# Batch 0 of a Fourier mixing and a gated feed-forward block: half-size even sums, another order of loads, joins and E copies in the head of the kernel

## The chip, the cores and the metric

The kernel runs on one core of one Trainium2 chip. The metric is the device time in microseconds (us) of one execution: the median of three runs before the change is 1908.64 us (1908.24 to 1908.96). A core has TensorE (PE, with the weight load PEld beside it), VectorE (DVE), ScalarE (ACT), GpSimd (POOL) and SyncE (SP), which here issues nearly all of the transfers, and 16 DMA engines.

## What is computed

```python
def _attn_ref(x):                       # x: (8, 3008, 256), float32
    X = np.fft.fft(x, axis=1)
    X = np.fft.fft(X, axis=2)
    return X.real.astype(np.float32)

def _moe_ref(x, w_gate, w_val, w_out):  # x: (24064, 256); d_ff = 1536
    gate = 1.0 / (1.0 + np.exp(-(x @ w_gate)))
    val = x @ w_val
    return (gate * val @ w_out).astype(np.float32)
```

The second takes the result of the first, reshaped to rows of 256. The three weights arrive as float64 and are converted on the chip.

## The kernel before, in words

The transform over the sequence is done with cosine and sine tables (`stab`, held in SBUF as `ST[0]` and `ST[1]`, 128 partitions x 6 sets q x 753 columns: 377 for even frequencies, 376 for odd ones). The rows of a batch are first folded on VectorE (`fold_ops`, `half_rows` for batch 0), so that 128 x 6 points remain; point number 6p + q lies in partition p and set q. TensorE then sums over the partitions, once per set: 128 feature columns as weights, 377 or 376 table columns as the moving operand. Sums over even sets go to one PSUM bank (`ev`) and over odd sets to another (`od`). `places` writes their sum to the low frequencies and their difference to the mirrored high ones (`ends` 0 and 1). The results are `pk` (cosine) and `qk` (sine). The one feature column that is its own mirror, "E", gets its own sums with one-column weights, whose outputs lie in four groups of 32 partitions of one PSUM bank (`e_sums`); its row goes to the DRAM tensor `ed`, and is read back broadcast to all partitions as `ek` (`e_load`, `e_rows`).

The feature transform is not applied to the data: it is merged into the gate and value weights. For each of 18 weight blocks, `weight_load` brings 0.5 MB of float64; `weight_parts` (two ACT operations), `weight_join` (two `tensor_scalar` and one `scalar_tensor_tensor` on VectorE, one add on GpSimd) make float32 of it; `weight_use` calls `merge`, which is four matmuls with the table `dt` into a bank `ps` and two ACT copies to `G2` and `G1`, each block giving two of the 12 hidden chunks of gate or value. One first row of `G2` per hidden chunk goes to `ge`.

Then comes the main loop, one step i per batch, frequency chunk of 252 and hidden chunk of 128 (576 steps). A step multiplies `pk` (`front_a`) and `qk` (`front_b`) with `G1` and `G2` into a bank `pf` with two halves, gate and value; for the first five steps E is added by a matmul with the row `e0`, from step 5 on an ACT operation seeds the bank with `ek` times `ge`. `gate_a` and `gate_b` make the gated product `h` on ACT and VectorE; `back` multiplies it with the output weights into `po` banks, five steps later. In the first 13 steps, the blocks of weights not yet merged are converted and merged beside this.

All queues are written out by hand, in program order for each engine: the scheduler is manual, so an engine does its instructions in the order in which the code names them, and waits on semaphores for what they read. `at(i, f)` puts a piece of work behind step i; `gap`, `pre`, `join`, `use` and `spare` put it at other places of a step. At most eight of SP's transfers are in flight: the ninth waits for the first.

The head, before step 0, is what the change rewrites. Its order before: load weight blocks 0 and 1, then rows and tables of sets 0 and 1, 2 and 3, 4, 5 (`load_rows`, `load_table`, L192 and L195), with the odd columns of the sine table last; convert and merge blocks 0 and 1; fold, sum and place set by set in the order of `SLICES`; convert blocks 2 and 3; the places of E, cosine and sine.

Of the kernel before, what the change touches and what calls it, by code (L numbers as in the profile page):

```python
# [8 lines left out]
F32 = mybir.dt.float32  # L9
# [3 lines left out]
ALU = mybir.AluOpType  # L13
# [40 lines left out]
NQ = 6  # L54
NP = 128
# [26 lines left out]
def kernel(  # L82
# [10 lines left out]
    nc = tc.nc  # L93
    B, _, _, _, D = xf.shape
    F = moe_w_gate.shape[1]
# [36 lines left out]
    def mm(o, l, r, start, stop):  # L132
        nc.tensor.matmul(o, l, r, start=start, stop=stop, skip_group_check=True)  # L133

    def bank(name, other=None):
        if other is not None:
            return pso.tile([P, 512], F32, name=name, tag=f"po{other}")
        return psx.tile([P, 512], F32, name=name, tag="x")
# [49 lines left out]
    table = const.tile([2, 1], F32, name="table")  # L188
    ed = dram.tile([B, NK + 1], F32, name="ed")

    def load_rows(q, n):
        nc.sync.dma_start(out=X[0][0:NP, :, q : q + n], in_=xf[0, :, :, q : q + n])  # L192

    def load_table(t, q, n, lo=0, hi=NE + NO):
        nc.sync.dma_start(out=ST[t][0:NP, q : q + n, lo:hi], in_=stab[:, t, q : q + n, lo:hi])  # L195

    NQ4 = NE // 4 + 1
    TILES = [(g, par, par * HP + g * TB) for g in range(2) for par in range(2)]
# [199 lines left out]

    WO = {}

    turns = itertools.count()

    def weight_use(j):
        w, c = jobs[j]
        if w == 2:
            WO[c] = WS.pop(j)
        else:
            merge(WS.pop(j), w, c, (4, 2, 3)[next(turns) % 3] if j > 1 else None)

    def merge(ws, g, c, other):  # L410
        cs = slice(c * WC, (c + 1) * WC)
        ps = bank("ps", other)
        for h in range(2):
            for t in range(2):
                mm(ps[:, h * WC : (h + 1) * WC], dt[:, t, h * HD : (h + 1) * HD], ws[:, t, :],
                   h == 0 and t == 0, t == 1)
        nc.scalar.copy(G2[:, g, cs], ps[:, WC : 2 * WC])
        nc.scalar.copy(G1[:, g, cs], ps[:, 0:WC])
        for f in range(c * WC // P, (c + 1) * WC // P):
            nc.sync.dma_start(  # L420
                out=ge[:, g, f : f + 1], in_=G2[0:1, g, f * P : (f + 1) * P])
# [60 lines left out]
    TURN = {}  # L482
    MORE = {}

    SLICES = ((0, 1), (2, 3), (4,), (5,))

    def fold_ops(b, nq):
        x4 = X.pop(b)
# [82 lines left out]
        else:  # L571

            def half_rows(q):
                even, odd = slice(0, 4, 2), slice(1, 4, 2)
                point(nc.vector, even, odd, q)
                first(nc.vector, even, odd, q)
                for blk in range(2):
                    across(nc.vector, blk, q)
                v, r = x4[:, 0:2, q], x4[:, 2:4, q]
                for to, op in ((r, ALU.subtract), (v, ALU.add)):  # L580
                    nc.vector.tensor_tensor(to[:, :, :, 1:HD], v[:, :, :, 1:HD], v[:, :, :, D - 1 : HD : -1],
                                            op=op)
                nc.vector.memset(r[:, :, :, 0:1], 0.0)
            ops += [lambda q=q: half_rows(slice(q[0], q[-1] + 1)) for q in SLICES]
        for blk, (v, r) in enumerate(parts):
            if b and blk:
                W[b, blk] = v[:, :, HD:D], r[:, :, HD:D]
# [4 lines left out]

    PQE = {}

    def half(b, w, d, blk, sn, other=None):


        c0, n = ((0, NE), (NE, NO))[blk]
        ev, od = [bank(name, other and other[i])[:, 0:n] for i, name in enumerate(("ev", "od"))]

        def sums(*qs):
            for q in sorted(qs, key=lambda q: q % 2):
                mm((ev, od)[q % 2], w(q), ST[int(sn)][0:NP, q, c0 : c0 + n], q < 2, q >= NQ - 2)

        def then():
            a = evp.tile([P, NE], F32, name="a", tag="a")[:, 0:n]
            nc.scalar.copy(a, ev)
            return lambda: places(d, blk, sn, a, od)
        return sums, then

    def places(d, blk, sn, ev, od, ends=(0, 1)):
        if 0 in ends:
# [64 lines left out]
        for t in PQE[b]:  # L677
            nc.vector.memset(t[:, NK:], 0.0)

    def seq_group(b, blk, what, other=None):  # L680
        return half(b, lambda q: W[b, blk][what][:, q, :], PQE[b][what], blk, what == 1, other)


    def e_load(b):
        nc.sync.dma_start(out=x8[:, b - 1], in_=xf[b, :, :, :, HD : HD + 1])

# [4 lines left out]
        tt(x8[:, :, 1], x8[:, :, 0], x8[:, :, 2], op=ALU.add)  # L691
        tt(x8[:, :, 3], x8[:, :, 0], x8[:, :, 2], op=ALU.subtract)

    E0 = []

    def e_sums(m=B - 1):


        ps = bank("pe", NB - 1)
        at_ = lambda blk, par: slice((2 * blk + par) * TB, (2 * blk + par) * TB + m)  # L700

        def sums(*qs):
            for q in qs:
                for blk in range(2):
                    c0, n = ((0, NE), (NE, NO))[blk]
                    w = x8[:, :, 1 + 2 * blk, q] if m > 1 else W[0, blk][2][:, q]
                    mm(ps[at_(blk, q % 2), 0:n], w, ST[0][0:NP, q, c0 : c0 + n], q < 2, q >= NQ - 2)

        def even():
            er = op.tile([P, NK + 1], F32, name="er", tag="os")[0:m]  # L710
            if m == 1:
                E0.append(er)
            nc.vector.memset(er[:, NK:], 0.0)
            if m > 1:
                a, e1 = (evp.tile([P, NE], F32, name="a", tag="a")[0:m] for _ in range(2))
                o1 = a
            else:
                a, e1 = (zp.tile([P, 2 * CH], F32, name="z", tag="z")[0:m, 0:NE] for _ in range(2))
                o1 = app.tile([P, 2 * CH], F32, name="ae", tag="ae")[0:m, 0:NE]
            nc.scalar.copy(a, ps[at_(0, 1), 0:NE])  # L720
            nc.scalar.copy(e1[:, 0:NO], ps[at_(1, 0), 0:NO])

            places(er, 0, True, a, ps[at_(0, 0), 0:NE])

            def rest():
                nc.scalar.copy(o1[:, 0:NO], ps[at_(1, 1), 0:NO])

            def last():
                places(er, 1, False, e1[:, 0:NO], o1[:, 0:NO], (0,))

            def end():
                places(er, 1, False, e1[:, 0:NO], o1[:, 0:NO], (1,))
                nc.sync.dma_start(out=ed[1:] if m > 1 else ed[0:1], in_=er)
            return rest, last, end
        return sums, even

    def e_joint():
        sums, even = e_sums()
        sums(*range(NQ))
        return even()  # L740

# [206 lines left out]
    nc.gpsimd.memset(nil, 0.0)  # L950
    nc.scalar.activation(table, nil[:, 0, 0:1], AF.Sigmoid)
    nc.gpsimd.dma_start(out=zero, in_=nil)
    nc.scalar.dma_start(out=dt, in_=dtab.rearrange("(c p) d -> p c d", p=P))
    load_x(0)
    for j in range(2):
        weight_load(j)
    load_rows(0, 2)
    load_table(0, 0, 2)
    load_rows(2, 2)
    load_table(1, 0, 2, 0, NE)  # L960
    load_table(0, 2, 2)
    load_rows(4, 1)
    load_table(0, 4, 1)
    load_rows(5, 1)
    weight_load(2)
    load_table(1, 2, 2, 0, NE)
    load_table(0, 5, 1)
    load_table(1, 4, 2, 0, NE)
    load_table(1, 0, NQ, NE)
    for j in (3, 5, 6, 8, 9, 4, 7):  # L970
        weight_load(j)

    e0 = shared["qk"][:, 4 * WC : 4 * WC + CH]
    nc.gpsimd.memset(e0, 0.0)
    weight_parts(0)
    weight_parts(1)
    weight_join(0)
    weight_join(1)
    warm = bank("warm", 2)
    for i in range(4):  # L980
        mm(warm[:, 0:WC], dt[:, 0, 0:P], dt[:, 0], True, True)
    weight_use(0)
    weight_use(1)
    seq_start(0)

    cos = [seq_group(0, blk, 0, (2 * blk, 2 * blk + 1)) for blk in range(2)]
    e_, e_even = e_sums(1)
    sin = [seq_group(0, 0, 1)]
    for q, f in zip(SLICES, fold_ops(0, 2), strict=True):
        f()  # L990
        e_(*{1: (0, 1), 5: (2, 3, 4, 5)}.get(q[-1], ()))
        sin[0][0](*{5: (3,)}.get(q[-1], ()))
        cos[0][0](*q)
        cos[1][0](*q)
        sin[0][0](*{1: (0, 1), 4: (2,), 5: (4, 5)}.get(q[-1], ()))
    places_c = [cos[blk][1]() for blk in range(2)]
    weight_parts(2)
    weight_join(2)
    rest, *ends = e_even()
    rest()  # L1000
    for f in ends:
        f()
    for f in places_c:
        f()
    nc.scalar.copy(e0[0:1], E0[0][:, 0:CH])
    weight_parts(3)
    weight_join(3)
    sin.append(seq_group(0, 1, 1, (0, 1)))
    sin[1][0](*range(NQ))
    for j in range(KEEP, KEEP + 3):  # L1010
        weight_load(j)
    places_s = [group[1]() for group in sin]
    for f in places_s:
        f()
    e_rows(0)

    per = NFT * len(chunks)
    side, mid, gap, spare = {}, {}, {}, {}

    def at(i, *fs):  # L1020
        side.setdefault(i, []).extend(fs)
# [21 lines left out]
    for i, f in zip((1, 2, 2, 2, 3, 4, 4, 4, 5, 6, 6, 8, 8, 8, 9, 9, 9, 9, 10, 10, 10, 11, 11), quarter_x(1), strict=True):  # L1043
        at(i, f)
    at(i0 + 1, lambda: load_x(1))
    for b in range(1, B):
        at(20 + b, lambda b=b: e_load(b))
    at(3 * i0, e_fold)
# [37 lines left out]
    def first_ends():  # L1086
        one, two = quarter_ends(1, 1), quarter_ends(1, 0)
        for i, f in zip((55, 65, 65, 66, 66, 67, 67, 68, 68, 69, 69, 70, 70, 71, 71, 72, 73, 74, 75, 76),
                        one[0] + two[0] + one[1] + two[1], strict=True):
            gap.setdefault(i, []).append(f)  # L1090
    at(16, first_folds)
    at(3 * i0 + 14, lambda: seq_start(1))
    for blk in range(2):
# [152 lines left out]
```

## Time and profile before

| | us |
|---|---|
| median of three runs | 1908.64 |
| the profiled execution | 1909.15 |
| its span | 1907.4 |
| PE busy in the span | 1895.6 |
| first matmul of the first `pf`, from the span's start | 33.05 |
| VectorE, ScalarE, GpSimd busy | 1520.6, 1353.2, 1543.4 |

The granted clock is full throughout. Times in the profile count from the span's start. "L133" is the helper `mm`, so matmuls are told apart by their tiles; one call of `mm` shows as two instructions, and "x8" is four calls.

### The profile page before, as it was taken

To read this page: it belongs to the slowest core of one execution; us is meant where nothing else is said; L and a number is where in the kernel's file an instruction comes from. 1 tells how busy PE (TensorE), PEld (TensorE's weight loads), DVE (VectorE), ACT (ScalarE), POOL (GpSimd) and SP (SyncE) were. 2 spreads that over 40 slices of the span, in tenths; PEclk is the share of its full clock that TensorE was granted. 3 is DMA by queue.
4 is the path that set the end of the run, shared out by engine and by line. 5 is a ranking of instruction groups with operands and counts; after the bars stand their busy time and mean duration, and the time that the engine had idled before them with its cause. 6 is when DMAs were issued, how large, how long until landed. Compare 5 with 4: busy or idle time off the path is not lost.

```text
span 1907.4 us, 36057 instructions
## 1 busy us (share of the span) xinstructions
PE 1895.6 (99%) x11836; PEld 1756.6 (92%) x11836; DVE 1520.6 (80%) x3375; ACT 1353.2 (71%) x3235; POOL 1543.4 (81%) x2733
## 2 busy tenths in 40 slices
PE   8999999999999999999999999999999999999999
PEld 5788999999999999999999999999999999999998
DVE  7678888878979778897788878888788777977775
ACT  4777777777777777777777777677767777777775
POOL 2489879987999779997799878999789986877770
PEclk9999999999999999999999999999999999999999
DMA  8446221212022121211211212122120110010001
GB/s 315 120 134 80 71 89 51 72 33 81 21 64 54 31 87 32 62 41 37 89 39 48 45 39 81 40 52 58 30 74 17 36 37 15 15 25 17 15 18 30
DMA packets 197333, 109.33 MB, mean 57 GB/s; under 512 B 134823, under 2 KB 188818, under 8 KB 195354
## 3 DMA queue, kind: packets, MB, share of 16 engines
q1 hardware_dynamic: 196568, 106.50, 21.1%
q8 instruction: 95, 1.56, 0.3%
q14 instruction: 92, 0.75, 0.1%
q10 hardware_dynamic: 546, 0.51, 0.1%
q0 software_dynamic: 32, 0.00, 0.0%
HBM read 71.24 MB, written 47.87 MB: 62 GB/s over the span
## 4 chain that ended last, share of the span: by engine, by line
PE 94%; DMA 2%; SPq 1%; POOL 1%; ACT 1%; DVE 0%; issue 0%; ACTq 0%; POOLq 0%
PE pf L133 49%; PE po L133 41%; PE sum L133 2%; DMA rtab<-in_stab_dram 1%; PE ps L133 1%; POOL sf L824 1%; DMA st<-in_stab_dram 1%; SPq L206 1%; DMA raw<-in_moe_w_val_dram 0%; PE od L133 0%; POOL x L507 0%; SPq L192 0%; SPq L375 0%; PE pe L133 0%; PE ev L133 0%
## 5 line engine op out<-in xcount | busy, mean ns | idle before, releaser
L824 POOL TENSOR_TENSOR sf<-h,sf 128x168 f32<-128x168 f32 (+1 forms) x1104 | 621.0, 582 | 79.5 <-DVE h L818 75.9
L824 POOL TENSOR_TENSOR sf<-h 128x168 f32<-128x168 f32 (+1 forms) x920 | 519.3, 584 | 159.8 <-DVE h L818 158.0
L133 PE MATMUL pf<-qk,G 128*128 128x252 f32 (+1 forms) x2304 | 583.4, 376 | 0.9 <-ACT ae L787 0.8
L133 PE MATMUL pf<-pk,G 128*128 128x252 f32 (+1 forms) x2304 | 582.7, 376 | 0.0
L772 ACT ACTIVATE pf<-ek,ge 128x252 f32<-128x252 f32 (+1 forms) x1142 | 538.2, 471 | 23.2 <-DMA ge<-G 3.0
L133 PE MATMUL po<-sf,wf 128*128 128x168 f32 (+1 forms) x2944 | 508.3, 305 | 0.0
L787 ACT ACTIVATE ae<-pf 128x504 f32<-128x504 f32 (+1 forms) x576 | 338.8, 588 | 218.7 <-PE pf L133 217.2
L133 PEld LDWEIGHTS pf<-pk,G 128*128 128x128 f32 x2304 | 435.9, 190 | 53.3 <-ACT pf L772 1.5
L133 PE MATMUL po<-h,wf 128*128 128x168 f32 (+2 forms) x2584 | 461.3, 307 | 0.0
L133 PEld LDWEIGHTS po<-sf,wf 128*128 128x128 f32 x2944 | 453.4, 190 | 8.0
L818 DVE TENSOR_TENSOR h<-pf,z 128x252 f32<-128x252 f32 (+1 forms) x576 | 240.4, 417 | 274.0 <-ACT pf L815 270.5
L802 DVE TENSOR_TENSOR z<-ae,pf 128x504 f32<-128x504 f32 (+1 forms) x576 | 384.6, 668 | 83.1 <-ACT h L801 79.1
L908 DVE TENSOR_TENSOR c<-c 128x168 f32<-128x168 f32 (+1 forms) x920 | 438.7, 500 | 3.3
L133 PEld LDWEIGHTS pf<-qk,G 128*128 128x128 f32 x2304 | 410.6, 190 | 32.3 <-ACT ae L787 2.1
L133 PEld LDWEIGHTS po<-h,wf 128*128 128x128 f32 x2584 | 410.4, 190 | 17.8 <-issue 0.9
L801 ACT ACTIVATE h<-pf 128x252 f32<-128x252 f32 (+1 forms) x576 | 216.9, 376 | 146.3 <-PE pf L133 129.0
L815 ACT ACTIVATE pf<-z 128x252 f32<-128x252 f32 (+1 forms) x576 | 214.3, 372 | 116.4 <-DVE h L814 114.5
L814 DVE TENSOR_TENSOR h<-h,pf 128x252 f32<-128x252 f32 (+1 forms) x576 | 232.9, 404 | 0.0
L824 POOL TENSOR_TENSOR sf<-sf 128x168 f32<-128x168 f32 (+1 forms) x184 | 101.7, 553 | 14.4
L824 POOL TENSOR_TENSOR sf<-sf,h 128x168 f32<-128x168 f32 (+1 forms) x184 | 110.1, 598 | 0.0
L891 ACT COPY c<-po 128x504 f32<-128x504 f32 (+1 forms) x138 | 78.5, 569 | 0.0
L918 DVE STREAM_TRANSPOSE os<-c 128x256 f32<-128x256 f32 x188 | 76.5, 427 | 0.1
(158 smaller groups left out, 876.4 us busy)
## 6 DMA issues: line engine op xcount, KB each, us to landing
x<-xr SPq DMA_DIRECT2D x14, 1536.0 KB
out_dram<-os SPq DMA_DIRECT2D x376, 56.0 KB
xr<-in_xf_dram SPq DMA_DIRECT2D x105, 128.0 KB
x<-x SPq DMA_DIRECT2D x112, 96.0 KB
xr<-in_xf_dram SPq DMA_DIRECT2D x14, 384.0 KB
ek<-ed SPq DMA_DIRECT2D x40, 126.0 KB
out_dram<-os SPq DMA_DIRECT2D x288, 7.0 KB
xr<-in_xf_dram SPq DMA_DIRECT2D x21, 124.0 KB
```

What stands on the lines that cost most here:

```text
L133: nc.tensor.matmul(o, l, r, start=start, stop=stop, skip_group_check=True)
L772: nc.scalar.activation(PF[i][:, g], EK[i // NFT], AF.Copy, scale=ge[:, g, f : f + 1])
L787: nc.scalar.activation(AP[i], PF[i], AF.Copy, scale=2.0)
L801: nc.scalar.activation(H[p][:, fh, 0:n], PF[i][:, 0], AF.Sigmoid)
L802: nc.vector.tensor_tensor(z[:, :, ::-1], AP.pop(i), PF[i], op=ALU.subtract)
L814: nc.vector.tensor_tensor(h[:, fh, 0:n], h[:, fh, 0:n], pf[:, 1], op=ALU.mult)
L815: nc.scalar.activation(pf[:, 0], z[:, 0], AF.Sigmoid)
L818: nc.vector.tensor_tensor(h[:, fh, n:], pf[:, 0], z[:, 1], op=ALU.mult)
L824: nc.gpsimd.tensor_tensor(block(p, dst), block(p, a), block(p, b), op=(ALU.subtract, ALU.add)[op])
L891: (nc.vector.tensor_copy if t == 1 or t == 3 else nc.scalar.copy)(C[0][:, 3 * t * R : 3 * (t + 1) * R], PO[t][:, 0 : 3 * R])
L908: nc.vector.tensor_tensor(t[:, dst * R : (dst + 1) * R], *v, op=(ALU.subtract, ALU.add)[op])
L918: nc.vector.transpose(os_[0][0][:, s, 0:nb, h, :], t[:, c0 : c0 + nb * TB])
```

## The change

The even sets are split by the mirror symmetry of the tables. Partitions with even number hold the rows of their own set; in partitions with odd number the rows of sets 0 and 2 are swapped by the loads (`load_rows`, in halves of 64 partitions), and likewise half of the table columns (`load_mixed`). A sum over set 0 or set 2 then gives, for 189 or 188 columns, only one of two banks x and y; set 4 is summed twice with a table that is zero in the partitions of the other parity (`apart`, in part of `wf`). `unfolded` makes the 377 and 376 even sums of them, with an add and a subtraction; `places` follows as before. E's sums are made in the same way (`e_first`).

The order of the head changes with it. Rows and tables of the even sets come first, as half tables, then sets 5, 1 and 3, then `dt` and the weight blocks. Warm-up matmuls run on zeros in place of `dt`. The unfolding and the low places of cosine come first, then the joins of blocks 0 and 1, then E, the sine unfolding, `e0`, the join of block 2 and the places of `qk`. E's sums are copied to free parts of `G1` and `G2`. Five of the mirrored places (`qk` of the first part, two of E, two of `pk`) move into steps 1 to 3, and with them E's store and the first `e_rows`. At step 35 `load_again` brings the whole even sets of the cosine table, which batches 1 to 7 need for E.

```diff
-    def load_rows(q, n):
-        nc.sync.dma_start(out=X[0][0:NP, :, q : q + n], in_=xf[0, :, :, q : q + n])
+    def load_rows(*qs):
+        for q in qs:
+            for ps, r in ((slice(0, NP, 2), q), (slice(1, NP, 2), 2 - q)) if q in (0, 2) else ((slice(0, NP), q),):
+                nc.sync.dma_start(out=X[0][ps, :, q], in_=xf[0, ps, :, r])
+    H0, H1 = NE // 2, NE + NO // 2
+    def load_table(t, q):
+        nc.sync.dma_start(out=ST[t][0:NP, q], in_=stab[:, t, q])
+    def load_mixed(t):
+        for ps, qs in ((slice(0, NP, 2), slice(0, 3, 2)), (slice(1, NP, 2), slice(2, None, -2))):
+            nc.sync.dma_start(out=ST[t][ps, 0:3:2, H0:H1], in_=stab[ps, t, qs, H0:H1])
+    def load_apart():
+        for h in range(2):
+            nc.sync.dma_start(
+                out=wf.rearrange("p g m n -> p g (m n)")[h:NP:2, h::2, 6 * WC : 6 * WC + NE], in_=stab[h::2, :, 4, H0:H1])
+    def load_again():
+        nc.sync.dma_start(out=ST[0][0:NP, 0:NQ:2], in_=stab[:, 0, 0:NQ:2])
...
-    SLICES = ((0, 1), (2, 3), (4,), (5,))
+    SLICES = (slice(4, 5), slice(0, 3, 2), slice(5, 6), slice(1, 2), slice(3, 4))
...
+    def unfolded(f, x, y, sn=False):
+        nc.vector.tensor_tensor(f[:, H0:H1], x[:, 0:NE], y, op=ALU.add)
+        two = [t[:, 1:NE].rearrange("p (b n) -> p b n", b=2) for t in ((y, x) if sn else (x, y))]
+        nc.vector.tensor_tensor(f[:, 0 : 2 * H1].rearrange("p (b n) -> p b n", b=2)[:, :, H0 - 1 :: -1], *two,
+                                op=ALU.subtract)
+    def seq_sums(what, x, y, od):
...
+        def even(*qs):
+            for q in qs:
+                for blk, (lo, n, to) in enumerate(cols):
+                    for h in range(2):
+                        if q == 4 or h == q // 2:
+                            tab = apart[what][h][0:NP, to : to + n] if q == 4 else ST[what][0:NP, q, lo : lo + n]
+                            add(2, (h, blk), (x, y)[h][:, to : to + n], w[blk][:, q], tab, blk == 0)
+        def odd(q, *blks):
+            for blk in blks or range(2):
+                lo, n = ((0, NE), (NE, NO))[blk]
+                add(3, blk + 2, od[blk][:, 0:n], w[blk][:, q], ST[what][0:NP, q, lo : lo + n])
...
+    load_rows(4, 0, 2)
+    load_apart()
+    for t in range(2):
+        load_mixed(t)
+    load_rows(5, 1)
+    load_table(0, 5)
+    load_rows(3)
+    load_table(0, 1)
+    load_table(1, 1)
+    nc.sync.dma_start(out=dt, in_=dtab.rearrange("(c p) d -> p c d", p=P))
+    weight_load(0)
+    load_table(0, 3)
+    weight_load(1)
+    load_table(1, 5)
+    load_table(1, 3)
+    for j in (2, 3, 5, 6, 8, 9, 4, 7):
         weight_load(j)
...
+    warm(bank("warm", 2), 12)
...
+    for q, n in (((4,), 3), ((0, 2), 0)):
+        next(folds)()
+        even(*q)
+        even_s(*q)
+        warm(od_c[0], n)
+    a, a_s = copy(), copy_s()
+    next(folds)()
+    odd(5)
+    for f in folds:
+        f()
+    pk = join(a)
+    HELD[0] = bank("ps")
+    od_s.append(bank("od"))
+    odd(1)
+    odd_s(1, 1, 0)
+    odd(3)
+    for blk in range(2):
+        pk(blk, 0)
+    weight_parts(0)
+    weight_join(0)
+    e_()
+    odd_s(5)
+    odd_s(3, 1)
+    weight_parts(1)
     weight_join(1)
+    er, e_end = e_unfold()
+    weight_parts(2)
     weight_use(0)
+    qk = join_s(a_s)
+    nc.vector.tensor_copy(e0[0:1], er[:, 0:CH])
+    HELD[1] = bank("ps", 3)
     weight_use(1)
+    odd_s(3, 0)
+    weight_join(2)
+    qk(0, 0)
+    qk(1, 0, 1)
+    weight_parts(3)
+    weight_join(3)
...
+    at(35, load_again)
...
+    at(1, lambda: qk(0, 1))
+    at(1, e_end)
+    at(2, lambda: e_rows(0))
+    for blk in range(2):
+        at(2 + blk, lambda blk=blk: pk(blk, 1))
```

## The prediction

> **What bounds it now.** I read the page first, then the chain of waits of the first 100 us, then the timeline and the stages. The page has PE busy 99% of the span; the chain says where it is not what ends last.
>
> ```profile
> PE 1895.6 (99%) x11836; PEld 1756.6 (92%) x11836; DVE 1520.6 (80%) x3375; ACT 1353.2 (71%) x3235; POOL 1543.4 (81%) x2733
> ```
>
> The chain of waits, in order of time (start, length, what):
>
> ```profile
> 1.26 5.86 DMA raw<-in_moe_w_val_dram
> ...
> 14.43 9.31 DMA st<-in_stab_dram
> ...
> 31.32 1.90 PE od L133 x6
> 33.21 4.25 PE pf L133 x20
> 37.46 3.45 PE ps L133 x16
> 40.91 0.90 PE pf L133 x4
> 41.81 1.73 PE ps L133 x8
> 43.54 1.70 PE pf L133 x8
> ```
>
> Up to 24 us the loads end last; from there to 95 us it is PE alone. So the whole change plays before the first `pf` (timeline: 33.05), and every us that `pf` starts earlier is a us gained, if PE then finds nothing late. The stages (DVE, ACT, POOL are the third to fifth pairs; then clock, DMA share, GB/s):
>
> ```profile
> 20.00:25.00 5.00, 4.90 (x22) 2.30 (x24) 4.54 (x15) 1.75 (x4) 0.00 (x0) 1.00 1.06 375
> 35.00:40.00 5.00, 5.00 (x25) 4.44 (x24) 3.73 (x6) 4.73 (x10) 1.36 (x1) 1.00 0.92 295
> ```
>
> The DMA engines are full (share 1.06) and DVE nearly so. Two more things, from the timeline: GpSimd holds VectorE up, and the third chunk has no slack on ACT.
>
> ```profile
> 36.59 0.43 DVE L393 TENSOR_SCALAR wqk<-wqk 128x512 int32<-128x512 int32 x1
> 37.88 1.36 POOL L397 TENSOR_TENSOR wqk<-wqk,raw 128x512 int32<-128x512 int32 x1 [3.43 <-ACT wf L383]
> 38.12 1.41 DVE L393 TENSOR_SCALAR wf<-wf 128x512 int32<-128x512 int32 x1
> 42.74 0.36 ACT L417 COPY G<-ps 128x256 f32<-128x256 f32 x1
> 43.00 0.37 ACT L418 COPY G<-ps 128x256 f32<-128x256 f32 x1
> 43.16 0.83 PEld L133 LDWEIGHTS pf<-pk,G 128*128 128x128 f32 x4
> ```
>
> The same DVE operation takes 0.43 alone and 1.41 when a join's GpSimd add runs. And the copies that write the merged weights for chunk rows 2 and 3 end at 43.37; PE's second `pf` matmul that needs them starts at 43.80 (43.37 plus one of 0.425). The margin is 0.43 us.
>
> **The change, part by part.**
>
> Loads. Two anchors of the chain give the rate: 1.31 MB had been issued through the weights that landed at 7.12 (1.26+5.86), 7.68 MB through the table that landed at 23.74, so 0.383 MB/us, and landing = 3.70 + MB/0.383. In the new order: rows q4 0.52 MB at 5.1, rows q0 and q2 1.57 at 7.8, the q4 half tables 1.96 at 8.8, both mixed tables 2.73 at 10.8, rows q5 12.2, q1 13.6, q3 15.9; cosine table q3 6.63 at 21.0; second weights 7.16 at 22.4; last table 7.93 at 24.4. Before, the last table was 9.61 MB, 28.8. The Trainium skill ("DMA: Bandwidth & Descriptors", Specifications) gives a core 358 GB/s from HBM; the stages show 375 to 407, so the measurement decides. By the page the cosine table would land 1.2 us later, and the time be 1.2 us more.
>
> PE. In `seq_sums`, for q0 and q2, eight sums of 0.63 become eight of half the columns: 2.5 us less. For q4, four of 0.63 become eight halves: nothing. The E sums (8 calls in 1.44 us, four column groups at once) stay near 2 us. The 15 warm-ups lie under loads. But the merges of the first two weights (1.73 each), which lay beside loads, now stand behind the sums: 3.5 us more on PE's path.
>
> DVE. Five memsets (0.34 or less each by the GpSimd one) end before rows q4 land: nothing. The folds regrouped: 5.2+4.1+2.5+2.5 become 2.52+4.11+3x2.52, the same. `unfolded` adds six operations of 0.46 to 0.53 (two each for cosine, sine and E); five end-places of 0.46 move into steps 1 to 3. The joins of weights 0 and 1 move from under the loads to behind `pk`.
>
> Now the queues in the new order. DVE: fold q4 5.1 to 7.6; q0 and q2 7.8 to 11.9; q5 12.2; q5, q1, q3 end at 14.7, 17.3, 19.8; cosine unfolding 20.8. PE's last cosine sums wait for that table: 21.0 to 22.3, plus 0.17 to drain. `pk` ends at 23.0. Join 0 takes 1.61 (0.46, 0.46, 0.69), to 24.5; its GpSimd add runs 24.65 to 25.95. Join 1's second operation waits for that, 1.0 more: 27.1. Its add ends at 28.55, merge 28.6 to 30.3, the held-back sine sum 0.63: **`pf` can start near 31.0, 2.0 earlier** than 33.05. The weights' parts and E's copies on ACT (20.0 to 27.6) end ahead of their readers.
>
> Does PE then find its operands? DVE goes on: E's four operations 2.3 (with 0.4 behind the GpSimd add), sine unfolding 1.0, copy of `e0` 0.2, join 2 1.6: 32.2. Three places of `qk`: 33.7, in time for the fifth `pf` pair at 34.4. Join 3 35.3; joins 5 and 6, each with 1.0 behind the add of the one before, 37.9 and 40.5; then `z` and `h` to 41.5 (before 41.20), the second sigmoid on ACT 41.95, weight parts 1.1, G copies 0.65: **43.7**. PE asks for that G at 43.80 less 2.0, 41.8, and waits about 2 us: ACT's queue has the copy behind the second sigmoid and the parts of weight 9, and that sigmoid behind VectorE's joins. So the 2.0 are given back. Worked through in the same way, the queues of before come out 0.2 early at that copy (43.14 against 43.37), so I take 43.95 for 43.80: **+0.15 us**.
>
> After it: DVE carries 2.3 us more in steps 1 to 3, but the bank that the fourth step needs is free at about 44 (PE asks at 47.65), so nothing. The E rows: before, the broadcast load was issued long ahead of its reader.
>
> ```profile
> 39.76 0.41 SPq L760 DMA_DIRECT2D ek<-ed  x1
> ...
> 54.31 0.97 ACT L772 ACTIVATE pf<-ek,ge 128x252 f32<-128x252 f32 x2
> ```
>
> Now the last place of E ends near 45.8, its store to `ed` follows at once on SP, and behind it wait two `ge` loads, two zero rows and 0.39 MB of batch 1's rows before the broadcast load goes out, near 51 (before, the rows went out at 50.03). Its landing is not shown; between 2.1 us (0.39 MB at 0.383, and the 1.1 that the stages show between bytes moved and landed at 7.12) and 5.6 (the one landing time on the page, of `zero`): 53.1 to 56.6 against 54.3 needed, with 0.9 of slack on PE (seed ends 55.28, PE uses it at 56.20). So 0 to 1.4; I take 0.1, near the lower end, which is of the same queue. The reload at step 35 is 1.16 MB, 3.0 us of engines that are 0.30 busy at 170 to 175; behind it on SP are out stores, `ek`, rows, and swaps of batch 1; E's joint sums (180.35) come 4 us after its landing. Nothing; uncovered it would cost its 3.0 to those.
>
> Sum: +0.15 + 0.1 = about 0.2. The profiled execution took 1909.15 (span 1907.4 and 1.75 around it), 0.5 above the median; I add the 0.2 to the median: 1908.8.
>
> **Rivals.**
>
> *PE keeps the gain* (1905.9). If the adds do not hold DVE up, three times 1.0 and 0.4 go: the copies are ready at 40.55, and PE's own queue decides: cosine sums to 22.3, E to 24.3, sine sums 1.9, two merges 3.5, the last sum 0.63, so `pf` at 30.3, 2.75 earlier. For it: a DVE operation with an operand in PSUM ran through beside an add (0.54 at 33.40). Against: joins have none in PSUM, and here they stand back to back.
>
> *That, and faster loads* (1904.7). DVE is ready for the cosine places at 20.8, a table at 19.8 would do, so loads can give 1.2 more: 4.0 in all. Against: it needs both, and 0.41 MB/us over 6.6 MB, the best of any stage.
>
> *E rows late* (1910.1): the 1.4 above, on top of +0.15.
>
> *The loads in alternate partitions are slow* (slower). The first ten loads hold 2.21 MB in halves of 64 partitions; no load of before has that shape. They take 5.8 us at 0.383. DVE's chain hangs on the table behind them, so each us they lose is lost at the end: at half the rate 5.8, 1914.6. It decides beyond a loss of 3.6, a rate under 0.235. For it: no row, and smaller loads with eight in flight. Against: rows q4 and q5, of 1 KB pieces, passed at 0.37. The Trainium skill ("SBUF — State Buffer", Summary: rules for kernel authors) asks for 128 partitions and one DMA instead of several when the transfer binds, which speaks against these halves; no run here shows it.
>
> **Numbers.** This kernel can tell 0.2% (3.8 us) from no change. Forecast, the gain returned: 0.50 (1907.6 to 1909.6 with what joins and copies may differ). PE keeps it, or most of it: 0.13. E rows late: 0.12. Both: 0.10, the faster case. Slow halves: 0.15, slower. So faster 0.10, same 0.75, slower 0.15. The range runs from 1905.4 (PE keeps 2.75, with 0.5 from loads) to 1912.6 (halves at 0.235), leaving out the fastest case and the worse part of the slow one.
>
> **What would show it.** `pf` starting near 31 and a PE wait of 1.5 to 2 us on ACT's G copy near 42 to 44; DVE rows of 1.4 in joins 1, 5, 6; the last cosine sum waiting on the table at 21. Wrong if `pf` runs through 44 without idle, if the cosine table lands after 23, or if the ACT seed of step 5 waits on `ek`.

## The result

| | before | after |
|---|---|---|
| median, us | 1908.64 (15 runs, 1908.09 to 1909.68) | 1912.44 (15 runs, 1911.18 to 1913.44) |
| the profiled execution, us | 1909.15 | 1911.48 |
| first `pf`, from the span's start | 33.05 | 33.24 |
| copy of `G` that step 2 waits for ends | 43.37 | 45.33 |
| first `ek` issued on SP | 39.76 | 53.46 |

The ratio of the medians is 1.0019, interval 1.0011 to 1.0027: slower by 3.8 us. That is inside the range (1905.4 to 1912.6), at its upper end, and 3.6 above the number.

**The profile after.** PE is as busy as before; the chain of waits (start, length, what) is no longer PE's from 24 us on.

```profile
PE 1899.5 (99%) x11870; PEld 1764.2 (92%) x11870; DVE 1525.3 (80%) x3394; ACT 1352.3 (71%) x3232; POOL 1544.1 (81%) x2733
```

```profile
0.74 0.70 SPq L194
...
7.43 0.61 SPq L203
8.09 5.44 DMA x<-in_xf_dram
...
22.25 0.94 issue
23.18 1.52 PE od L133 x4
...
27.19 1.41 DVE raw L412
```

Up to 8.09 SP's issues of eleven loads (rows q4 and the ten halves) end last, 0.60 to 0.70 us each; then the rows q5, which land at 13.5; then VectorE's folds; and PE starts the sums with the table of cosine set 3 at 23.18, where it was forecast to land at 21.0 (it landed at 23.1: SP's issue that needed its place among the eight in flight went out at 23.11). The stages (GB/s is the last column):

```profile
5.00:7.50 2.50, 2.50 (x9) 2.07 (x8) 2.36 (x7) 0.00 (x0) 0.00 (x0) 1.00 1.04 357
10.00:12.50 2.50, 2.50 (x17) 2.42 (x16) 2.40 (x5) 0.00 (x0) 0.00 (x0) 1.00 0.92 281
15.00:20.00 5.00, 3.24 (x13) 1.90 (x12) 4.72 (x15) 0.57 (x2) 0.00 (x0) 1.00 1.05 383
```

While the half loads move, the rate is 357, and 281 when they have run out; 0.383 MB/us, the rate of the forecast, comes only behind 15 us. Then the timeline:

```profile
33.24 1.01 PE L133 MATMUL pf<-pk,G 128*128 128x252 f32 x4
43.58 0.66 ACT L401 ACTIVATE wf<-wf 128x512 f32<-128x512 f32 x1
44.95 0.38 ACT L438 COPY G<-ps 128x256 f32<-128x256 f32 x1
45.38 0.69 PE L133 MATMUL pf<-pk,G 128*128 128x252 f32 x2 [1.23 <-ACT G L438]
53.46 0.55 SPq L829 DMA_DIRECT2D ek<-ed  x1
57.25 0.98 ACT L841 ACTIVATE pf<-ek,ge 128x252 f32<-128x252 f32 x2 [1.14 <-DMA ek<-ed]
58.28 1.12 PE L133 MATMUL pf<-pk,G 128*128 128x252 f32 x4 [0.23 <-ACT pf L841]
```

PE stands 1.23 us in front of step 2's copy of `G`, and the seed of step 5 waits for the row `ek`.

**Where the time goes.** I set the sigmoid of each step (L870, before L801) against that of before, from the span's start. The difference is called the offset below.

| step | 0 | 1 | 2 | 3 | 4 | 12 | 28 | 30 | 60 | 575 |
|---|---|---|---|---|---|---|---|---|---|---|
| offset of after, us | 0.19 | 1.63 | 2.57 | 1.73 | 2.92 | 2.95 | 2.94 | 2.02 | 2.06 | 1.93 |

So `pf` begins 0.2 late, the wait for `G` adds 1.4, and what follows from the wait for `ek` 1.2. (At step 2 ScalarE comes to its sigmoid later still, but PE's next matmuls are 1.7 late, no more.) PE's own matmuls tell the same: against before they start 0.19 late at step 0, 1.69 late behind step 2's `G`, 2.18 behind the seed of step 5, 2.41 behind that of step 6 and 2.93 behind that of step 8. The seeds of steps 6 and 8 wait for `ge` loads.

At steps 29 and 30 after regains 0.9, because it is the profiled execution of *before* that stands there:

```profile
146.54 0.20 ACT L256 COPY small<-st 32x6 f32<-32x6 f32 x1 [2.24 <-DMA st<-in_stab_dram]
147.84 1.12 PE L133 MATMUL pf<-qk,G 128*128 128x252 f32 x4 [0.60 <-ACT ae L787]
```

In after that wait is 1.3 at most and PE does not stand. Thus 1.9 at the last step, and 2.3 in the times of the two profiled executions (1911.48 and 1909.15). The medians are 3.8 apart because the profiled execution of after was 0.96 faster than the median of its kernel, and that of before 0.51 slower than its own. What makes the executions of one kernel differ by that much stays open, and with it the 0.9 between the offset of 2.95 and the 3.8: one trace of each kernel shows one execution.

### The profile page after: what moved, and what is told of

It reads as the page before. It is cut to its first block, busy times and chain, and to the rows that moved or that the text cites. A ratio compares the mean times of both kernels' runs of the same rounds, so it can differ in the third digit from the quotient of the medians.

```text
span 1909.5 us, 36162 instructions
## 1 busy us (share of the span) xinstructions
PE 1899.5 (99%) x11870; PEld 1764.2 (92%) x11870; DVE 1525.3 (80%) x3394; ACT 1352.3 (71%) x3232; POOL 1544.1 (81%) x2733
## 4 chain that ended last, share of the span: by engine, by line
PE 90%; DVE 3%; DMA 2%; POOL 2%; SPq 2%; ACT 1%; issue 1%; POOLq 0%; ACTq 0%; DVEq 0%
PE pf L133 47%; PE po L133 40%; PE sum L133 2%; POOL sf L893 1%; DMA rtab<-in_stab_dram 1%; SPq L225 1%; DVE c L977 0%; DVE z L871 0%; DMA ge<-G 0%; DMA x<-in_xf_dram 0%; ACT pf L884 0%; DMA st<-in_stab_dram 0%; ACT pf L841 0%; DVE h L887 0%; DMA xr<-in_xf_dram 0%
## 5 line engine op out<-in xcount | busy, mean ns | idle before, releaser
L870 ACT ACTIVATE h<-pf 128x252 f32<-128x252 f32 (+1 forms) x576 | 216.9, 377 | 147.2 <-PE pf L133 127.9
```

Source lines behind the costliest of these rows:

```text
L870: nc.scalar.activation(H[p][:, fh, 0:n], PF[i][:, 0], AF.Sigmoid)
```

## The experiments

Twelve runs, each timed beside the kernel before on the same chip, where the median of before was 1908.44 to 1908.51. "Offset" is that of steps 12 to 28. (The expectations say 3.0 for the changed kernel's 2.95.) "PE at G" and "PE at E" are PE's idle time ahead of step 2's second `pf` and of the first `pf` behind the `ek` seed.

| kernel | median | ratio to before, interval | `pk` starts | `pf` | PE at G | PE at E | offset |
|---|---|---|---|---|---|---|---|
| after | 1912.44 | 1.0011 to 1.0027 | 24.09 | 33.24 | 1.23 | 0.23 | 2.95 |
| after_again | 1912.41 | 1.0012 to 1.0030 | 24.39 | 33.53 | 1.21 | 0.49 | 3.22 |
| two_queues | 1911.64 | 1.0008 to 1.0026 | 23.23 | 32.38 | 1.21 | 0.24 | 1.86 |
| rows_first | 1911.86 | 1.0008 to 1.0026 | 23.33 | 32.48 | 1.22 | 0.44 | 2.36 |
| table_first | 1911.51 | 1.0010 to 1.0027 | 22.76 | 33.02 | 0.89 | 0.40 | 2.92 |
| unfold_between | 1917.71 | 1.0035 to 1.0060 | 24.56 | 40.05 | 0.52 | 0.16 | 9.17 |
| unfold_free | 1911.91 | 1.0008 to 1.0026 | 23.99 | 33.54 | 0.43 | 0.24 | 2.35 |
| whole_sums | 1913.92 | 1.0018 to 1.0040 | 26.33 | 35.65 | 0.44 | 0.50 | 4.75 |
| parts_later | 1912.17 | 1.0011 to 1.0028 | 23.75 | 32.89 | 0 | 1.53 | 2.73 |
| ek_first | 1910.62 | 1.0003 to 1.0021 | 23.73 | 32.88 | 1.23 | 0 | 1.16 |
| two_waits | 1909.67 | 0.9997 to 1.0015 | 23.90 | 33.04 | 0 | 0 | 0.62 |
| best1 | 1909.48 | 0.9995 to 1.0013 | 22.17 | 31.73 | 0.42 | 0 | -0.22 |
| best2 | 1908.50 | 0.9993 to 1.0011 | 23.84 | 33.41 | 0 | 0 | 0.66 |

Most intervals of the modified kernels overlap: the medians alone seldom tell them apart, and what follows rests on offsets and rows. An idle time of PE can be less than what PE loses: at the seed of step 5 after shows 0.23 idle, but its matmuls fall 0.5 further behind.

**after_again: how much is one execution.** No edit.

> The changed kernel as it is, once more: a second trace of it, to see which of the offsets belong to the kernel and which to one execution. Two kernels with the same head showed pf at 33.24 and 32.6 by the landing of the cosine table, so: pf between 32.5 and 33.3, offset of steps 12 to 28 between 2.3 and 3.0, the wait for E's row again; the stall of 0.9 that the trace of before has at step 29 is absent or present, and the time is 0.9 apart by it. Median 1912.4.

The two waits are there again. Rows q5 are folded from 14.43 (13.55 in the first trace), and the offset is 3.22, just above what was expected. The five runs with the loads and joins of after (after, after_again, parts_later, ek_first, two_waits) start `pf` between 32.88 and 33.53. So offsets that differ by up to about 0.6 may be the landing of one execution, and only larger ones, or ones with their row, are read as the edit's.

### What makes the loads late

**two_queues.**

```diff
-                nc.sync.dma_start(out=X[0][ps, :, q], in_=xf[0, ps, :, r])
+                (nc.scalar if ps.start else nc.sync).dma_start(out=X[0][ps, :, q], in_=xf[0, ps, :, r])
```
(and the same in `load_mixed` and, by `h`, in `load_apart`)

> The changed kernel with one edit: the loads of odd partitions (rows q0 and q2, set 4 of the tables, the mixed tables: five of the ten half loads) are issued from ACT's queue, the others stay on SP. Theory 1 (issue): SP needs 0.60 to 0.70 us for each small load, eleven stand ahead of rows q5, so these go out at 8.09 only and the engines run short of work; that is what makes the table of cosine set 3 land at 23.1 where 21.0 was forecast. Then rows q5 land near 12.3 (13.55 in the changed kernel), the table near 21.4, pk starts 22.4 (24.09), pf 31.6 (33.24), the copy of G that step 2 waits for ends near 43.7 (45.33), the offset of the sigmoids of steps 12 to 28 against the kernel before falls from 3.0 to about 1.4, and the median by 1.6. Theory 2 (halves of 64 partitions are slow themselves): rows q5 and the table land where they did, within 0.4, and the time is the same. Theory 3 (VectorE's joins under GpSimd's adds set the pace, not the loads): the table is earlier, pf is not.

Half right: `pk` is 0.86 earlier where 1.7 was expected, the offset 1.86 where 1.4 was, and rows q5 are only 0.2 earlier. The chain of this kernel says why:

```profile
2.19 6.08 DMA x<-in_xf_dram
8.28 5.04 DMA x<-in_xf_dram
```

SP had its turn by then, but rows q5 are issued when an earlier half of rows has landed, at 8.28 (8.09 in after): with two issuers it is the eight transfers in flight that hold them back. The Trainium skill ("DMA: Bandwidth & Descriptors", Issuing engines are not separate DMA queues) says that a second issuing engine saves only the time of initiating. The trace does not speak against it: no more was saved than the 1.7 us expected from the issue time, and of that 0.2 for rows q5.

**rows_first.** `load_rows(4, 0, 2, 5)` first, `load_rows(1)` where q5 and q1 stood.

> The changed kernel with one edit: rows q5 (0.52 MB, 128 partitions) are issued ahead of the six half tables. In the changed kernel the DMA engines moved 281 GB/s from 10.0 to 12.5, 350 to 385 around it: the small loads had run out before the bytes of rows q5, issued at 8.09, came. Issue theory: the small loads are now issued while rows q5 move; that stretch is above 340, VectorE folds q5 without a wait at 12.5 (13.55), the cosine table lands about 0.7 earlier, pk starts at 23.3 (24.09), the offset is 2.2. If halves are slow by themselves, the same bytes take the same time in any order: rows q5 early, the table where it was (23.1), pk within 0.3, time the same.

As expected: the stage from 10 to 12.5 rises from 281 to 372, the fold of q5 starts at 12.95 and waits for nothing, `pk` at 23.33.

```profile
7.50:10.00 2.50, 1.43 (x7) 0.92 (x5) 1.92 (x5) 0.00 (x0) 0.00 (x0) 1.00 1.08 358
10.00:12.50 2.50, 1.62 (x9) 1.48 (x10) 2.36 (x6) 0.00 (x0) 0.00 (x0) 1.00 1.06 372
```

With halves in flight the engines move 358 to 372 here, against 376 to 390 behind 15 us, and against 401 to 415 in the same two stretches of whole_sums (below), whose loads are whole: halves of alternate partitions cost some 10% in these executions, not half. That rival falls. Of the 2.1 us that the table is late, this order regains 0.8 in `pk`: that part was the gap in the supply behind the small loads. The offset, 2.36, is 0.6 lower, no more than executions differ.

**table_first.** `load_table(0, 3)` ahead of `dt` and `weight_load(0)`.

> The changed kernel with one edit: the table of cosine set 3 is loaded ahead of dt and the weights of block 0 (0.78 MB) instead of behind them. Theory 1 (what is late is the table, by its place in a queue that lost about 2 us to issue): the table lands near 21.1, pk starts at 22.3 (24.09), when VectorE is through with folds and unfolding. Block 0 now lands near 23.1, its ACT parts end at 24.4, join 0 ends at 26.0 (26.8), so pf starts at 32.4 (33.24), the G copy of step 2 ends 0.8 earlier, at 44.5, the offset of steps 12 to 28 is 2.2 and the median 0.8 lower. Theory 3 (the table does not matter, the joins do, wherever pk ends): no change beyond 0.3.

A miss: the table is earlier (`pk` 22.76), but `pf` starts at 33.02 where 32.4 was expected, and the offset is 2.92 where 2.2 was. Step 1 is 1.09 late in place of 1.63, and that gain is lost again: PE's matmuls fall 0.7 further behind at the `ek` row (0.5 in after), and 0.9 at step 8, whose seed waits for a `ge` load (0.5 in after; PE stands 0.60 at 74.36 for it). These transfers did not come earlier by as much as PE did.

**whole_sums: the halving undone, all else kept.**

```diff
-    load_apart()
-    for t in range(2):
-        load_mixed(t)
+    for t, q in ((0, 4), (1, 4), (0, 0), (0, 2), (1, 0), (1, 2)):
+        load_table(t, q)
...
+                for blk, (lo, n) in enumerate(((0, NE), (NE, NO))):
+                    add(3, blk, (x, y)[blk][:, 0:n], w[blk][:, q], ST[what][0:NP, q, lo : lo + n])
```

> The changed kernel with the halving undone and all else kept (order of loads, joins, deferred places, E copies in G1 and G2): whole rows and whole tables of the even sets, 12 sums of 377 or 376 columns for the even sets of each kind in place of the half ones, ScalarE copies the even sums (two a kind, four for E) and nothing is unfolded on VectorE; no reload at step 35. If the halving buys what the sum of the prediction gave it: 1.16 MB more ahead of the cosine table, 3.0 us at 0.385, less what the whole loads regain of the 2 us lost to issue: the table lands near 24.6 (23.1). VectorE loses the 1.1 of the cosine unfolding ahead of it without use, so pk starts at 25.6 (24.09) and pf at 34.7 (33.24). Behind that the E and sine unfoldings (2.15) are gone, so the G copy of step 2 ends near 44.8 (45.33): the offset of steps 12 to 28 is about 2.4, that is, the halving pays nothing, because the step that decides is VectorE's queue. If the table decides alone, the offset is 4.5.

```profile
26.33 1.18 DVE L656 TENSOR_TENSOR pk<-wf,od 128x377 f32<-128x377 f32 x2 [2.44 <-PE od L133]
```

The second reading holds: the table decides. `pk` is 2.2 later than in after and the offset 1.8 higher (4.5 was expected in all, 4.75 came), although VectorE has two unfoldings less behind it: those gave back 0.6 at the copy of `G` (1.6 late there). So within this order the halving is worth some 1.8 us in these executions, by its bytes; the order around it, without the halving, stands 4.75 behind the kernel before.

### What follows from the late table

**unfold_between.** `qk = join_s(a_s)` moved ahead of `weight_parts(1)`.

> The changed kernel with one edit: the sine unfolding (two VectorE operations of 0.55 with an operand in PSUM) stands between joins 0 and 1 instead of behind E's unfolding. Theory 1 with the lock of the prediction: the second operation of join 1 takes 0.43 instead of 1.40, join 1 ends where it did (29.3), pf starts at 33.2 as before, and all of VectorE's later work is 1.0 earlier: the G copy of step 2 ends at 44.4 (45.33), the offset of steps 12 to 28 falls from 3.0 to 2.0. If the 1.40 is not the GpSimd add's doing but the operation's own behind another one, join 1 ends 1.1 later, pf starts at 34.3, and the time is up to 1 longer.

Neither theory: 5.3 us slower than after by the medians, 6.2 by the offset. VectorE stood in front of the unfolding, and PE behind it:

```profile
31.09 0.55 DVE L616 TENSOR_TENSOR u<-u,a 128x377 f32<-128x377 f32 x1 [3.81 <-PE ps L133]
35.22 3.78 PE L133 MATMUL ps<-raw,dt 128*128 128x256 f32 x8 [4.23 <-POOL raw L416]
```

The buffer that it writes (`hp`, three slots) holds the raw weights of block 0, which the merge on PE reads; moved ahead of join 1, it held join 1 and all behind it. A second loss came on top: PE idled 4.23 us, and from 33.9 to 40.7 its granted clock was 0.50, so that this merge took 3.78 us in place of the 1.99 of after. The position of an instruction in the changed kernel had a reason that its operands' names do not show.

**unfold_free.** The same, with the result in a free part of `G1` (and one copy of E's sums moved to another row of `G1` to make room).

```diff
-            f = hp.tile([P, 6 * WC], F32, name="u", tag="h") if what else wf[:, 0].rearrange("p m n -> p (m n)")
+            f = G1.rearrange("p g n -> p (g n)")[:, F - NE - NO :] if what else wf[:, 0].rearrange("p m n -> p (m n)")
```

> The changed kernel with the sine unfolding between joins 0 and 1, as in the run before, but written to a free part of G1 instead of the buffer that holds the raw weights of block 0 until their merge has read them (in that run VectorE waited 3.8 us for the merge, in front of join 1). Lock theory: the GpSimd add of join 0 now runs beside operations with an operand in PSUM, the second operation of join 1 takes 0.43 instead of 1.40, join 1 ends at 29.4 as in the changed kernel, pf starts at 33.2, VectorE is 1.0 earlier from E on, the G copy of step 2 ends at 44.4 (45.33), the broadcast load of E's row goes out up to 1.0 sooner, and the offset of steps 12 to 28 against the kernel before is 2.0 or less (3.0). If VectorE's queue does not set that copy: no change.

```profile
26.63 0.54 DVE L616 TENSOR_TENSOR G<-u,a 128x377 f32<-128x377 f32 x1
26.86 1.28 POOL L416 TENSOR_TENSOR raw<-raw 128x512 int32<-128x512 int32 x1 [24.52 <-DVE raw L414]
28.46 0.43 DVE L412 TENSOR_SCALAR raw<-raw 128x512 int32<-128x512 int32 x1
```

That GpSimd's add holds VectorE up (the lock of the expectations) is shown: beside the same add, operations with a PSUM operand take their 0.54, and join 1's second operation 0.43 in place of 1.40 (0.33 of the add's rest falls on its first, 0.76 for 0.42). PE's wait for `G` falls from 1.23 to 0.43, as expected 0.8 to 1.0. The offset is 2.35, above the 2.0 expected, and `pf` starts at 33.54 in place of 33.24. The Trainium skill ("SBUF — State Buffer", Who interferes with whom) says that a VectorE operation with at most one SBUF input, outside the two-port modes, does not contend with GpSimd, while `tensor_scalar` in such a mode blocks; these rows agree.

### The two waits

**parts_later.** ScalarE's two parts of block 9 behind step 1's copies of `G` (`at(1, pre[1].pop(0))`).

> The changed kernel with one edit: ScalarE does the two parts of weight block 9 (1.2 us) behind the G copies of step 1's merges instead of ahead of them. If those copies are late because they stand behind these parts (43.65 to 44.82 in the changed kernel, PE idle 1.23 ahead of 45.38), the first pair of copies ends near 44.3, PE's wait there falls to 0.2, and step 2 is 1.0 earlier. What is late next by the theory is the broadcast load of E's row: its store follows VectorE and its issue follows SP, which do not move by as much, so the PE wait ahead of step 5 grows from 0.2 to about 0.7 and the offset of steps 12 to 28 is 2.3 to 2.5 (3.0), median 0.5 to 0.7 lower. If the copies wait for the merges or for VectorE: no change.

```profile
57.09 0.98 ACT L841 ACTIVATE pf<-ek,ge 128x252 f32<-128x252 f32 x2 [2.45 <-DMA ek<-ed]
58.13 1.12 PE L133 MATMUL pf<-pk,G 128*128 128x252 f32 x4 [1.53 <-ACT pf L841]
```

The wait for `G` is gone, and PE's wait for `ek` grew from 0.23 to 1.53: what the first gives, the second takes (0.7 was expected there). The offset, 2.73, is a little above 2.3 to 2.5, and the median 0.3 lower where 0.5 to 0.7 was expected.

**ek_first.** The broadcast load ahead of step 2's zero rows and rows of batch 1.

```diff
-    at(2, lambda: e_rows(0))
+    side[2].insert(0, lambda: e_rows(0))
```

> The changed kernel with one edit: the first broadcast load of E's row is issued ahead of step 2's zero rows and rows of batch 1 on SP, not behind them. If the seed of step 5 waits for it (57.25 in the changed kernel, PE at 58.28 where its own work would have ended at 57.89): issue near 51.5 instead of 53.46, landing near 55.3, no PE idle there, the offset grows no more than 0.1 from step 2 to step 5; of the 1.3 that the offset grows between steps 2 and 12 at least 0.4 goes, so steps 12 to 28 show 2.6 or less. If the later waits on ge and ACT follow from it, all 1.3 goes: 1.7. If they come from VectorE being late, only the 0.4.

```profile
51.18 0.55 SPq L829 DMA_DIRECT2D ek<-ed  x1
...
55.64 0.98 ACT L841 ACTIVATE pf<-ek,ge 128x252 f32<-128x252 f32 x2
```

Issued 2.3 earlier, the row no longer holds the seed, and all of the growth behind step 1 goes: 1.28 at step 1, 1.16 at step 12 (1.63 and 2.95 in after). In after PE lost only 0.5 us at this seed. The rest is ScalarE's: behind the seed lie a sigmoid, four weight parts and the copies of `G`, and ScalarE was 1.2 later at all of them; the `ge` loads that read `G` went out later by it, and the seeds of steps 6 and 8 waited for them.

**two_waits.** Both edits.

> The changed kernel with two edits that were run one by one: the parts of block 9 behind the G copies of step 1, and the first broadcast load of E's row ahead of step 2's rows. Loads, joins, deferred places and reload are the changed kernel's. If its 3.0 us at steps 12 to 28 are these two waits and next to nothing else, the offset is that of step 0 (-0.4 to 0.5 by the landing of the table, 0.2 in the first trace) plus 0.2 to 0.4 for what is left of the G wait: 0.0 to 0.8, and the median is 1.8 to 2.6 lower, near 1910.0. If more hangs on VectorE's late chain (ge, seeds), the offset stays above 1.2.

0.62, and 1909.67: 1.2 above before where after is 3.8 above it, so 2.6 gained, the upper end of what was expected. These two waits are most of the loss of the changed kernel, 2.3 of its offset of 2.95; the 1.2 that is left lies inside this run's interval.

### A version that beats both?

**best1** (rows_first, table_first, unfold_free, ek_first) and **best2** (best1 with parts_later, and three deferred places moved between joins 3, 5 and 6):

> Four edits together: rows q5 ahead of the half tables, the cosine table q3 ahead of dt and block 0, the sine unfolding between joins 0 and 1 into the free part of G1, the first broadcast load of E's row ahead of step 2's rows. If the waits add as the theories say: cosine table near 20.5, pk from 21.4; block 0 lands at 22.6, join 0 ends 25.4, join 1 28.0, pf starts at 31.4; the G copy of step 2 ends at 42.9 (43.37 in the kernel before); no wait for E's row; offset against the kernel before 0.0 to -0.5 at steps 12 to 28, median 1908.0 to 1908.6. If the order of the queues only moves the waits, 1 to 2 us above that.

> The four edits of the best so far, the parts of block 9 behind the G copies, and three of the places deferred to steps 1 to 3 moved between joins 3, 5 and 6, where GpSimd's adds hold VectorE up (0.97 each) and operations with a PSUM operand do not wait. If the waits add: PE's last wait of the head (0.42 at step 2) goes, z of step 0 is no later (the places fill the locks), offset -0.8 to -1.2 at steps 12 to 28 against -0.39, median 1908.2 to 1908.9. If PE has no slack there any more, or the locks do not fill: -0.4 as before.

best1 starts `pf` at 31.73 and is 0.22 ahead of before at steps 12 to 28 (the -0.39 of the second text is not the number of these steps); its median is 0.9 above what was expected. PE's matmuls show where the early `pf` went: 1.32 ahead at step 0, 0.63 ahead behind step 2's `G`, 0.23 ahead behind the seed of step 8.

best2's profiled execution was the slowest of its eleven: its `pk` came 1.7 later than in best1, whose loads are the same. The granted clock shows why (third figure from the end; the first pair is PE; best1, then best2):

```profile
12.50:15.00 2.50, 2.50 (x16) 2.35 (x15) 2.30 (x8) 0.00 (x0) 0.00 (x0) 1.00 1.04 367
12.50:15.00 2.50, 2.50 (x10) 2.50 (x9) 2.40 (x7) 0.00 (x0) 0.00 (x0) 0.50 1.08 379
```

In best2 it was 0.50 from 12.2 to 15.6 us, behind a wait of PE for the first half table; 3.4 us at half clock are 1.7 us of PE's work. So the offset of 0.66 says nothing of the added edits; PE has no wait for `G` or `ek` in it. In best1, too, the five executions with a mean granted clock of 0.999 are the five slowest (1909.57 to 1910.38), and the six at 1.000 took 1907.54 to 1909.48. best2's median is that of before, 1908.50 against 1908.49. Neither beats before by what can be measured.

## Why the prediction was right and wrong

The case was right, the size not: the change gives no gain, and 3.8 us lies at the bound of 3.8 that the text set for no change. That the time still lies in the range is luck: the range reached to 1912.6 for halves at 0.235 MB/us, and they moved at 0.36; what filled it was two waits that the sum had put at 0.25 together. These are the two terms that were mis-sized. The offset of 2.95 against the 0.25 of the sum makes 2.7 of the 3.6 us missed; the 0.9 between offset and medians stays open.

*Landing law.* It took 3.70 + MB/0.383 from two anchors of a queue of large loads. The order after it has ten small halves in front: PE had the cosine table at 23.18, not 21.0, and rows q5 were folded at 13.55, not 12.2. All behind it follows at its distance: `pk` ends 25.3 (23.0), `pf` starts 33.24 (31.0). The 2.0 us of earlier `pf` were lost there, not given back at step 2. Only best1, with an earlier table, shows the case that the text forecast: of the 1.3 us by which its `pf` is early, step 2 takes 0.7 back. The forecast of where the queues stand *relative to the table* held: folds, join 0, the 1.40 of joins 1, 5 and 6, the merges.

*G copy.* The wait came at the place and by the mechanism forecast (second sigmoid behind the joins, then the parts of block 9), 1.23 where about 2 was said; but with `pf` not earlier it is a loss, not the return of a gain: 1.4 in the offset (1.5 by PE's matmuls) in place of 0.15.

*E rows.* Bounded at 0 to 1.4, taken as 0.1; it was 1.2, near the upper end. Two things were missed. The load was issued at 53.46, not near 51, behind E's store (48.43) and the loads of step 2, which follow VectorE's lateness: the last place of E ended at 47.4, not 45.8. And the bound reasoned with PE's slack of 0.9 at the seed, while what mattered was what ScalarE had queued behind the seed. This was the rival "E rows late", on top of a table 2.1 late.

*Rivals.* "PE keeps the gain" falls: the adds do hold VectorE up. "Faster loads" falls too, the table was 2.1 later than forecast. The slow halves fall as they were priced (358 to 372 GB/s in rows_first, not 0.235 MB/us), though a lag of the loads, 2.1, did come, by issue and by the gap behind the small loads (0.9 and 0.8 in `pk`, with two_queues and rows_first). The reload at step 35 costs nothing that shows: the offset at step 36 (2.08) is that of step 30 (2.02). The deferred places were not tried by themselves.

*Signs named.* "`pf` near 31" failed. "The table lands after 23" and "the seed of step 5 waits on `ek`" were both listed as what would make it wrong, and both came.

## What to carry to other kernels

A landing law fitted to large loads did not hold for a queue of small ones: count the issue time of each, the transfers in flight, and what is ready to move when the small ones run out. When a step is deferred, follow its result to the first reader's *queue*: a late row on ScalarE delays all that stands behind the reader, not the matmul alone. Before moving an instruction, look whose data its output buffer still holds. When PE stands longer in the new order, look at the granted clock behind it before reading the time as the edit's.

## What was not expected of the hardware

The landing of the same loads moved by up to 0.9 us between two executions of one kernel (rows q5 folded at 13.55 and 14.43). A broadcast load of one row of 252 numbers to 128 partitions took 3.8 us from issue to the seed (53.46 to 57.25; 3.72 in the chain of two_queues), near the middle of the bounds of the prediction. A `ge` column load took 1.92 at 50.29 and 4.00 at 69.77 in the chain of after, and 3.87 to 4.37 in the chains of the others.

Of the 14 traces two show a granted clock of 0.50 in the head: best2, where PE had stood 2.17 us (up to 10.90), for 3.4 us, and unfold_between, where it had stood 4.23 us (up to 35.22), for 6.8 us. In rows_first PE stood 1.95 us and the clock stayed at 1.00. None of the 98 executions of before that ran beside the experiments had a mean granted clock under 1.000; 36 of the 122 of the experiments' kernels did. Warm-up matmuls that last until the first sums were not tried.
